# Loading the first nine raw parts of w_in one part per transfer instead of three

## The chip, the cores and the metric

The kernel runs on one core of one Trainium2 chip. The metric is device time in microseconds (us) of one execution. Smaller is better.

## The reference

Two blocks follow each other. The first is a gated delta rule over 4 batches, 8 heads, 768 positions and a head width of 48: for each position the normalised key reads the 48x48 state, and the state gets a rank-one correction.

```
k_n = k / (norm(k) + 1e-6)
for t in range(768):
    y[t]  = q[t] @ state
    v_old = state.T @ k_n[t]
    state = state + beta[t] * outer(k_n[t], v[t] - v_old)
```

The heads are then laid side by side, which gives x with 3072 rows and 384 columns, and the second block is `out = gelu(x @ w_in) @ w_out` with `gelu(h) = h * sigmoid(1.702 h)`. `w_in` is 384x2048 and `w_out` is 2048x384. Both weights arrive as 64-bit floats, because the scale that makes them is a 64-bit number; q, k, v and beta are 32-bit.

## The kernel before

**Tiling.** The 768 positions are cut into 6 chunks of 128, and each pair of chunk and batch is one of 24 units. A unit's keys are turned (`psT`, `kT`), multiplied with each other (`psG`, `G`), and `G` is written to DRAM and read back in another layout (`Nd<-G`, then `NT<-Nd`). `invert` solves the small triangular systems on VectorE: it works in `NT`, `YB` and products `P`, ends in `YS`, and sends that through DRAM too (`Yd<-YS`, then `XB<-Yd`). TensorE uses `XB` in `psU`, ScalarE copies the result to `US`, TensorE makes `psR` from it, and VectorE subtracts `psR` from `V`. That step repeats for four blocks of 32 positions. The results, `xT`, feed the second block: `ph` is x @ w_in, `gT` is its gelu, `po` is the product with w_out.

**Weights.** Each raw 64-bit part is loaded into a place that is not needed yet (the tail of `w_out`, which is why the profile calls its destination `w_out`) and then converted to 32 bits on VectorE by `from_double` (L182 to L194). `w_in` has 12 parts: part `3*g + j` is column group g (512 columns) and contraction third j (128 rows). The list `x_rows` (L204) says how the 128 partitions of one part are filled: partitions 0 to 47, 48 to 63, 64 to 111 and 112 to 127, so four transfers, each with rows of 512 doubles (4 KB). `together_with` (L226) makes the first nine parts travel three at a time: in one call of `fetch` (L234) four transfers load three parts, and within a partition the three parts lie side by side. Parts 9, 10 and 11 travel alone.

**Order of the work around the change.** The loads of the first nine parts are issued by SyncE, from `ahead(1, sync)` (L875, parts 0 to 2, after the keys) and `ahead(2, sync)` (L899, parts 3 to 8, after q, v and more keys and ahead of the first `invert`). `sync` is the pinned form of the SyncE issue: pinned instructions keep the order in which the program names them on their engine. Parts 9 to 11 and all of w_out are issued by GpSimd. Part 0 is converted in L876 on VectorE after `normalize_first` for the first four keys, parts 1 and 2 in L890, then comes the first `invert` (L900), `normalize_first` for three more keys, and the conversion of the next parts (L902 and `weights` in each slot, counts in `WB`). TensorE is kept awake by `warm` matmuls (`ps_warm`) on data that nobody reads. Slots -1 to 5 run `slot`, those from 6 on run `woven`; in slots 2 to 5 VectorE, ScalarE and TensorE instructions are not pinned, and the framework's scheduler sets their order when the program is built.

Of the kernel before, what the change touches and what calls it, by code (L numbers as in the profile page):

```python
# [18 lines left out]
def kernel(  # L19
# [107 lines left out]
    for blk in range(NB):  # L127
# [10 lines left out]
        out=YB, in_=YB, compare_op=ALU.not_equal, fill=1.0, base=0,  # L138
# [27 lines left out]
    def from_double(dst, raw, n, alone):  # L166
# [37 lines left out]
    x_rows = [  # L204
        (ct * DP + o, (ct * NP + i) * D, m, step)
        for ct in range(2)
        for o, i, m, step in ((0, 0, D, D), (D, KC, XR, XR))
    ]
# [3 lines left out]
    def stage(part):  # L212

        if part < parts_in:
            at = part % (2 * KC) * 2 * N_IN
            return at, at + 2 * N_IN
        f = part - parts_in
        if f >= FC - 2:
            return None
        depth = 2 if f < 2 or f >= 8 else 4  # L220
        if f >= 12:
            depth = 1
        at = FC * DM // (2 if f < 2 else 1) - (f % depth + 1) * 2 * DM
        return at, at + 2 * DM

    def together_with(part):  # L226

        return list(range(part, part + (KC if part < 3 * KC else 1)))
# [5 lines left out]
    def fetch(part, dma):  # L234

        if part < parts_in:
            j, f0 = part % KC, part // KC * N_IN
            parts = together_with(part)
            shape, src = (len(parts), N_IN), moe_w_in[:, f0 : f0 + N_IN]
            dst = w_in[:, j : j + len(parts), f0 : f0 + N_IN]  # L240
        else:
            parts = [part]
            shape, src = (1, DM), moe_w_out
            dst = target(part)
        if src.dtype != F32:
            if (s := stage(part)) is None:
                raw = wk.tile([128, *shape, 2], I32, tag="xT", name="raw", bufs=3)
            else:
                words = slice(s[0], stage(parts[-1])[1])
                raw = w_out.rearrange("p f d -> p (f d)")[:, words].bitcast(I32)  # L250
                raw = raw.rearrange("p (j n o) -> p j n o", j=shape[0], o=2)
            for i, p in enumerate(parts):
                stages[p] = raw[:, i]
                if s is not None:
                    taken[p] = stage(p)
            dst = raw.bitcast(src.dtype).rearrange("p j n o -> p j (n o)")
        if part < parts_in:
            for p, r, m, step in x_rows:
                row = src[r + j * step : r + j * step + m]
                dma(  # L260
                    out=dst[p : p + m],
                    in_=bass.AP(
                        row.tensor, row.offset, [row.ap[0], [row.ap[0][0] * step, len(parts)], row.ap[1]]
                    ),
                )
        else:
            r = (part - parts_in) * 128
            dma(out=dst if src.dtype == F32 else dst[:, 0], in_=src[r : r + 128, :])
        return parts

    def target(part):
        if part < parts_in:
            j, f0 = part % KC, part // KC * N_IN
            return w_in[:, j, f0 : f0 + N_IN]
        return w_out[:, part - parts_in, :]
# [394 lines left out]
    def ahead(n, dma=nc.gpsimd.dma_start):  # L670

        while n > 0 and waiting and free(waiting[0]):
            staged.extend(fetch(waiting.pop(0), dma))
            n -= 1
# [228 lines left out]
    for n in range(-1, len(units) + 1):  # L903
        in_order[0], now[0] = n < HB or n >= W, n
        step = slot if n < W else woven
# [32 lines left out]
```

## Time and profile before

| What | Value |
|---|---|
| median of 4 runs | 826.1 us (823.93 to 828.8) |
| the profiled execution's own time | 827.8 us |
| its span | 826.1 us |
| TensorE matmul busy | 771.9 us (93% of the span) |
| VectorE busy | 485.1 us (59%) |
| DMA on SyncE's and ScalarE's queue (q1) | 139488 packets, 41.96 MB, 24.8% of 16 engines |
| w_in loads from SyncE | 6 of 576 KB, 12.2 us to landing; 6 of 192 KB, 12.8 us |
| w_in loads from GpSimd | 6 of 192 KB, 4.4 us; 6 of 64 KB, 4.1 us |

The span runs from the first to the last instruction of the profiled execution; its own time is 1.7 us longer, which lies around the span. A busy share is an average over stages with different limits. TensorE has idle time mostly in the first eighth of the span, where the weights arrive; later it is busy nearly all the time.

### The profile page before, as it was taken

Reading aid. Unit: us, or ns where it says so; the run is one execution under the profiler, and the core shown is the slowest. Engines: PE = TensorE matmul, PEld = TensorE weight load, DVE = VectorE, ACT = ScalarE, POOL = GpSimd, SP = SyncE. Lnnn points to the kernel's source line nnn. Section 1 sums busy time; section 2 is a strip of 40 time slices with the busy share of each in tenths; the row PEclk is TensorE's granted clock in tenths of the full one; section 3 lists DMA queues with packets and bytes.
Section 4 is the critical chain, followed back from the end, with each engine's and each line's share of the span. In section 5 each row is a group of like instructions: output and inputs, shape, how many; then the busy total and the mean of one; then the engine's idle time right before and its main releaser. Section 6 shows DMA issues by size and latency. Waiting matters only on the chain.

```text
span 826.1 us, 18734 instructions
## 1 busy us (share of the span) xinstructions
PE 771.9 (93%) x8100; PEld 581.2 (70%) x8100; DVE 485.1 (59%) x1037; ACT 230.5 (28%) x499; POOL 131.3 (16%) x138
## 2 busy tenths in 40 slices
PE   8438699989989999999999999999999999999998
PEld 7327598556766876876867867867868768677684
DVE  6998889687876665675666667666656730100000
ACT  2303543242322332332322422322322323212120
POOL 2103120242021121222122122112201000000000
PEclk9559988987969999999999999999999999999999
DMA  9996632622124223123214204213222010000000
GB/s 148 201 157 148 171 94 69 174 67 77 46 42 101 53 57 85 38 56 92 62 21 101 62 22 101 53 33 89 52 56 47 11 41 11 11 16 1 24 1 19
DMA packets 147314, 55.96 MB, mean 68 GB/s; under 512 B 114336, under 2 KB 143232, under 8 KB 147232
## 3 DMA queue, kind: packets, MB, share of 16 engines
q1 hardware_dynamic: 139488, 41.96, 24.8%
q0 software_dynamic: 2752, 10.62, 4.3%
q10 hardware_dynamic: 4992, 2.20, 1.0%
q8 instruction: 63, 1.03, 0.5%
q14 instruction: 19, 0.16, 0.1%
HBM read 33.13 MB, written 20.45 MB: 65 GB/s over the span
## 4 chain that ended last, share of the span: by engine, by line
PE 77%; DVE 9%; issue 6%; DMA 5%; POOL 2%; ACT 1%; SPq 0%; DVEq 0%; POOLq 0%; ACTq 0%
PE po L105 28%; PE ph L105 25%; PE psY L105 5%; PE psU L105 4%; PE psQ L105 3%; PE ph L638 3%; DVE P L105 2%; PE psG L105 2%; DMA Nd<-G 2%; PE psR L105 2%; PE ps_warm L154 2%; DVE YB L105 2%; PE psT L105 1%; DMA w_out<-in_moe_w_out_dram 1%; PE psG L367 1%
## 5 line engine op out<-in xcount | busy, mean ns | idle before, releaser
L105 PE MATMUL po<-w_out,gT 128*128 128x384 f32 x704 | 239.3, 490 | 0.0
L105 PE MATMUL ph<-xT,w_in 128*128 128x256 f32 x966 | 222.1, 384 | 0.3
L105 PEld LDWEIGHTS ph<-xT,w_in 128*128 128x128 f32 x966 | 180.3, 191 | 30.9 <-issue 2.3
L105 PEld LDWEIGHTS po<-w_out,gT 128*128 128x128 f32 x704 | 130.1, 190 | 82.6 <-issue 1.9
L105 DVE TENSOR_TENSOR V<-V,psR 64x384 f32<-64x384 f32 (+1 forms) x80 | 44.4, 555 | 192.4 <-PE psR L105 191.6
L105 DVE TENSOR_TENSOR P<-NT,YB 64x18 f32<-64x18 f32 (+25 forms) x171 | 82.3, 481 | 4.5
L105 ACT ACTIVATE gT<-ph 128x512 f32<-128x512 f32 x81 | 48.2, 595 | 115.9 <-PE ph L105 115.8
L105 DVE TENSOR_REDUCE YB<-P 64x6 f32<-64x18 f32 (+25 forms) x171 | 72.6, 425 | 5.5
L105 ACT COPY US<-psU 32x384 f32<-32x384 f32 x80 | 37.6, 470 | 123.7 <-PE psR L105 116.9
L533 POOL TENSOR_SCALAR_AFFINE_SELECT M<-M 128x1024 f32<-128x1024 f32 x24 | 29.8, 1243 | 231.8 <-DVE M L105 162.9
L105 PEld LDWEIGHTS psU<-V,XB 32*32 32x32 f32 x1280 | 45.9, 105 | 29.3 <-issue 21.1
L105 PE MATMUL psU<-V,XB 32*32 32x48 f32 x1280 | 54.5, 203 | 3.7 <-DVE V L105 3.7
L105 PE MATMUL psR<-US,G 32*32 32x48 f32 x1920 | 52.8, 203 | 0.3 <-ACT US L105 0.3
L638 PE MATMUL ph<-xT,w_in 128*128 128x128 f32 (+1 forms) x282 | 51.0, 340 | 1.9 <-DMA xT<-last 1.9
L638 PEld LDWEIGHTS ph<-xT,w_in 128*128 128x128 f32 x282 | 43.6, 212 | 6.6 <-issue 2.9
L105 PEld LDWEIGHTS psR<-US,G 32*32 32x32 f32 x1920 | 44.6, 105 | 1.0 <-issue 0.5
L313 POOL TENSOR_TENSOR rn<-ssq,half 128x8 f32<-128x8 f32 x17 | 37.9, 2229 | 2.9 <-DVE ssq L311 2.9
L154 PE MATMUL ps_warm<-ident 128*128 128x256 bf16 x152 | 22.9, 318 | 16.0 <-DVE ps_warm L105 13.7
L90 POOL DMA_DIRECT2D KN<-in_k_dram x14 | 13.4, 955 | 153.0 <-PE psY L105 101.2
L105 ACT COPY o<-po 128x384 f32<-128x384 f32 x22 | 10.5, 479 | 77.7 <-PE po L105 55.8
L154 PEld LDWEIGHTS <-ident 128*128 128x128 bf16 x152 | 17.1, 114 | 20.4 <-issue 13.9
L105 DVE TENSOR_TENSOR P<-NT 64x256 f32<-64x256 f32 (+7 forms) x36 | 30.6, 849 | 0.3
(144 smaller groups left out, 869.8 us busy)
## 6 DMA issues: line engine op xcount, KB each, us to landing
Nd<-G SPq DMA_DIRECT2D x20, 512.0 KB, 3.5
w_out<-in_moe_w_out_dram POOLq DMA_DIRECT2D x14, 384.0 KB, 3.7
QP<-in_q_dram SPq DMA_DIRECT2D x24, 192.0 KB, 3.9
V<-in_v_dram SPq DMA_DIRECT2D x24, 192.0 KB, 2.9
out_dram<-o SPq DMA_DIRECT2D x24, 192.0 KB, 2.0
w_out<-in_moe_w_in_dram SPq DMA_DIRECT2D x6, 576.0 KB, 12.2
NT<-Nd SPq DMA_DIRECT2D x24, 128.0 KB, 2.7
Yd<-YS SPq DMA_DIRECT2D x24, 128.0 KB, 3.5
```

The costliest lines, as they stand in the source:

```text
L90: dma(out=dst[n % len(dst)][:, :, 0:D], in_=src[b, :, c * C : (c + 1) * C, :].rearrange("h p d -> p h d"),)
L105: return lambda *a, **kw: tc.keep_in_program_order(op(*a, **kw))
L154: pe.matmul(ps, lhsT=ones[:, 0:128], rhs=ones, start=True, stop=True)
L313: nc.gpsimd.tensor_tensor(rn, ssq, half, op=ALU.pow)
L367: pe.matmul(ps[h % 2][:, h // 2], lhsT=kT[r, h // 2, :], rhs=kT[r, h // 2, :], start=True, stop=True,)
L533: nc.gpsimd.affine_select(out=self.M, in_=self.M, compare_op=ALU.is_gt, fill=0.0, base=0, pattern=[[0, H], [1, 128]], channel_multiplier=-1,)
L638: pe.matmul(ph[:, u], lhsT=w_in[:, j, f * 128 : (f + 1) * 128], rhs=xT[:, j, t], start=(j == 0), stop=(j == KC - 1),)
```

## The change

For the parts that travel three at a time, the four transfers that each load three parts are replaced by twelve that each load one part, in the order part by part. The bytes, the rows of 4 KB, the places in SBUF, the issuing engine and the position in the program are the same. For parts 9 to 11 the loop runs once and issues the same four transfers as before.

```diff
         if part < parts_in:
-            for p, r, m, step in x_rows:
-                row = src[r + j * step : r + j * step + m]
-                dma(
-                    out=dst[p : p + m],
-                    in_=bass.AP(
-                        row.tensor, row.offset, [row.ap[0], [row.ap[0][0] * step, len(parts)], row.ap[1]]
-                    ),
-                )
+            for i in range(len(parts)):
+                for p, r, m, step in x_rows:
+                    dma(out=dst[p : p + m, i], in_=src[r + (j + i) * step : r + (j + i) * step + m])
         else:
```

Before, the rows of one partition (one for each of the three parts) follow each other in a transfer; after, each transfer has one row for each partition.

## The prediction

> **What bounds the kernel now.** I read the page's 40 slices first: TensorE stands at 9 tenths nearly everywhere after slice 5, and its gaps lie in the first 100 us, where all nine parts are loaded. So only the end of that opening can move the end of the kernel. I then read the timelines of VectorE, TensorE and SyncE in the two places where SyncE loads w_in, and the stretches of DMA beside them. Columns of a timeline: start, length, engine, line, operation, and in brackets the idle time before it and what ended it.
>
> First load (issued from 4.36 us):
>
> ```profile
> 4.36 2.08 SPq L105 DMA_DIRECT2D w_out<-in_moe_w_in_dram  x4
> 15.61 1.03 DVE L105 TENSOR_TENSOR KN<-KN,z 128x384 f32<-128x384 f32 x2
> 18.73 0.43 DVE L105 TENSOR_SCALAR w_in<-w_out 128x512 int32<-128x512 int32 x1 [2.09 <-DMA w_out<-in_moe_w_in_dram]
> 21.33 6.70 SPq L385 DMA_DIRECT2D NT<-Nd  x4
> 22.91 0.44 ACTq L105 DMA_DIRECT2D Nd<-G  x1
> 30.38 1.23 DVE L105 TENSOR_TENSOR NT<-NT,bI 128x1024 f32<-128x1024 f32 x1 [0.61 <-DMA NT<-Nd]
> ```
>
> VectorE is free at 16.64 and waits 2.09 us for w_in. It converts three parts until 29.77 and then waits again, 0.61 us, for NT. From 30.38 to 57.99 follows the first inversion, VectorE almost without a gap.
>
> Second and third load (issued 38.91 to 44.73):
>
> ```profile
> 38.91 5.82 SPq L105 DMA_DIRECT2D w_out<-in_moe_w_in_dram  x8
> 57.99 1.72 SPq L105 DMA_DIRECT2D Yd<-YS  x4
> 64.03 2.32 SPq L105 DMA_DIRECT2D XB<-Yd  x4
> 64.56 2.13 PE L105 MATMUL ps_warm<-ident 128*128 128x256 bf16 x18
> 66.64 0.86 PE L105 MATMUL psU<-V,XB 32*32 32x48 f32 x16
> 68.85 0.88 PE L105 MATMUL psR<-US,G 32*32 32x48 f32 x48
> 71.29 1.14 DVE L105 TENSOR_TENSOR V<-V,psR 32x384 f32<-32x384 f32 x2
> ```
>
> The loads land 8.9 to 19.5 us after their issue, the last at 63.8. Yd, on the same queue, lands at 64.0 to 64.8 (6.0 to 5.5 us), XB's first at 66.6. In VectorE's timeline there is no idle time from 57.9 to 72.9: three keys are normalised, part 3 and the start of part 4 are converted, and only then comes V.
>
> DMA at three times (columns: stretch, length, busy PE, PEld, DVE, ACT, POOL with counts, PE clock, DMA share, GB/s):
>
> ```profile
> 8.00:10.00 2.00, 2.00 (x20) 1.80 (x19) 1.76 (x9) 0.00 (x0) 0.00 (x0) 1.00 1.00 135
> 52.00:54.00 2.00, 0.00 (x0) 0.00 (x0) 1.97 (x3) 0.00 (x0) 0.00 (x0) 0.50 0.99 158
> 79.00:79.50 0.50, 0.50 (x7) 0.45 (x6) 0.50 (x2) 0.13 (x1) 0.50 (x2) 1.00 0.99 291
> ```
>
> The first two are loads of three parts, the third is a part that travels alone, from GpSimd's queue. All have 4 KB rows and engines busy throughout, yet the third moves about twice as much.
>
> [...] the 576 KB transfers run at 135 to 158 GB/s, those of 192 KB at 291. [...]
>
> **The change part by part.**
>
> *Transfer rate.* It gains. A part is 128 x 4 KB = 524 KB. Lower bound of the gain: none (150 GB/s stays, since SyncE's queue may not do what GpSimd's does); upper: 291. I take 291. The first load then flows from about 8.0 us, when the keys are in, for 1573 KB / 291 = 5.4 us and lands near 14.9 (1.5 us from the last byte to landing: the bytes ended at 17.0, the landing is 18.6) instead of 18.6. The second and third flow from about 42.5 for 10.8 us, landing near 55 instead of 63.8.
>
> *First stall.* The 2.09 us before the conversion go, at either rate: at 150 GB/s part 0 alone would land at 8.0 + 3.5 + 1.5 = 13.0, before VectorE is free at 16.64. VectorE then ends its conversions at 27.7. **NT is late next.** NT's last read is issued at 27.72, when the last Nd has landed, and lands 2.5 us later. Nd's last write starts at 22.91, as soon as ScalarE has copied G, behind TensorE and the normalised keys; none of that reads w_in. Nor do they share DMA: between 17.0 and 18.0 the engines are nearly idle (share 0.16 and 0.01), and the first Nd moves only from 18.3. So NT's arrival stays, the 0.61 us wait grows to 2.7, and the gain is 0.0. Bounds: 0 to 0.6 us; the whole 0.61 is had only if Nd comes sooner.
>
> *Issues on SyncE.* 8 more in the first load and 16 more in the other two, 0.436 us each by the median of the w_in rows: 3.5 us and 7.0 us. The first ends near 10 us; next on SyncE is NT at 21.33, which waits for Nd: hidden, with 11 us left. The others end near 51.7; next is Yd at 57.99, which waits for YS: hidden, 6.3 us left. If that cover were gone, Yd would be late one for one.
>
> *Eight transfers in flight.* After its eight issues SyncE's queue shows one wait of 3.1 us for a w_in load, from 44.73 to 47.8: exactly when the first of the eight landed, before it went on to wait 10.1 us for YS. I read this as: the ninth transfer waits for the landing of the first. Then the new loads wait for those eight ahead, so two parts are in flight. GpSimd's single transfers land after 3.6 to 4.7 us, which allows 1049 KB / 4.4 = 238 GB/s: 3146 KB in 13.2 us, until 55.7 and landed by 57.2, still ahead of Yd. At 150 GB/s part 7 would land near 61 and hold Yd's issue for 3 us; but Yd's bytes queue behind w_in to 62 today too, so it would land as it does now. Cost 0; bounds 0 to 0.6.
>
> *Yd and XB.* With w_in gone, Yd takes its usual 3.5 us (the page's median), XB is issued near 61.5 and its first lands near 64.1, 2.5 us sooner. **The warm matmuls are next.** TensorE runs them without a gap from 56.82 to 66.5, in pinned order ahead of psU; the wait for XB there is 0.2 us. So psU gains 0.2 us, and even that is lost at V, which waits for VectorE until 71.29 while psR ends near 69.7. Gain 0.0; bounds 0 to 0.2.
>
> *Conversions of parts 3 to 8* never wait for a load in the trace (the first is at 65.7); GpSimd's loads of parts 9 to 11 wait for VectorE to free their place (22.5 us at 68.44). Nothing moves.
>
> Sum: 0 + 0 + 0, with 0 to -0.8 from the covered pieces; I take -0.2. On the profiled execution's own time that is 827.8 to 827.6. That execution lies 1.7 above the median of 826.1, so the forecast is 825.9.
>
> **The rivals.**
>
> *Both stalls were real.* If NT came earlier with w_in, or the warm matmuls gave way, the end would gain 0.6 + 2.5 and, if VectorE's 2.09 us counted fully, up to 5 us: 821. For it: the chain of waits names Yd (5.49 us from 59.29). Against: VectorE has no gap there, so that piece is a bookkeeping of equals.
>
> *Another order in slots 2 to 5 (and of unpinned transfers elsewhere).* The scheduler sees twelve transfers where there were four and may place unpinned work differently between about 100 and 230 us. It decides when an Nd, NT, Yd or XB falls behind another unpinned transfer on SyncE that waits. Its price is read from waits of that region: psU waited 4.0 us for the XB issued at 226.77, and six xT transfers in a row hold the queue for 5.07 us. One such slip costs 4 to 5 us with TensorE otherwise full: 830.5, **slower**. It decides only where it puts more than the present wait ahead of psU. A lucky order removes the 4.0 us instead: 822. Nothing in the profile shows that the order will change.
>
> *The change doesn't speed the loads.* Then Yd lands as now, and the first stall still goes: 826.1, the same class.
>
> **How the numbers follow.** A difference under 0.5% (4.1 us) is about what a measurement of this kernel can tell from no change. Covered pieces as worked out, or no faster loads: 0.62. Faster by more than 4.1: 0.21 (0.10 both stalls real, 0.11 a better order). Slower by more than 4.1: 0.17, by order, with a few hundredths for Yd held on SyncE past 65. The likeliest case's own range is 823.5 to 828.5; the range to 8 in 10 reaches into both orders, 820.5 to 831.
>
> **What would show it.** Right: w_in transfers from SyncE landing in 4 to 7 us, DMA near 250 to 290 GB/s at 9 to 13 and 43 to 55 us, no wait for w_in before the first conversion but about 2.7 us for NT at 30.4; YS still at 56.7; Yd landing in about 3.5 us; psU still at 66.4 to 66.7, V at 71.3. Wrong: NT's product before 29.9, or psU before 66, or V before 71; SyncE's w_in issues past 58; or another order of instructions after 100 us.

## The result and the profile after

The changed kernel takes 823.1 us at the median of 43 runs (819.4 to 830.6), the kernel before 826.7 us of 64 runs (822.1 to 833.4). The ratio is 0.9959 with a 95% interval of 0.9945 to 0.9973: 3.4 us gained, 2.2 to 4.5. (The median of before was 826.1 when four runs were known.) Ratios and averages leave out the few runs that fell in a slower state of the chip. The profiled execution of after took 823.39 us with a span of 821.3 us, against 827.8 and 826.1 before. The mean granted clock is 0.952, against 0.948.

SyncE's timeline of after (start, length, engine, line, operation), as the prediction showed it of before:

```profile
4.25 6.80 SPq L105 DMA_DIRECT2D w_out<-in_moe_w_in_dram  x12
20.19 8.04 SPq L380 DMA_DIRECT2D NT<-Nd  x4
38.94 15.53 SPq L105 DMA_DIRECT2D w_out<-in_moe_w_in_dram  x24
58.66 1.71 SPq L105 DMA_DIRECT2D Yd<-YS  x4
60.64 2.66 SPq L105 DMA_DIRECT2D XB<-Yd  x4
```

XB is issued 3.4 us sooner than before (64.03), because Yd no longer lands behind w_in (1.9 to 2.3 us after its issue in place of 5.5 to 6.0). The DMA stretches of after (length, busy engines with counts, PE clock, DMA share, GB/s):

```profile
8.00:10.00 2.00, 2.00 (x21) 1.79 (x19) 1.76 (x9) 0.00 (x0) 0.00 (x0) 1.00 1.04 234
52.00:54.00 2.00, 0.00 (x0) 0.00 (x0) 2.00 (x4) 0.26 (x1) 0.00 (x0) 0.50 1.02 213
```

The DMA engines are as busy as before and move 234 GB/s in place of 135, and 213 in place of 158. Stretches of 2 us scatter; from 9 to 13 us it is 228 in place of 147, from 44 to 54 us 215 in place of 155. TensorE's clock is 1.00 in the first of the two stretches, where warm matmuls keep it busy for all 2.00 us, and 0.50 in the second, where it runs nothing. VectorE's timeline of after, in the opening:

```profile
16.52 0.42 DVE L105 TENSOR_SCALAR w_in<-w_out 128x512 int32<-128x512 int32 x1
...
30.45 1.22 DVE L105 TENSOR_TENSOR NT<-NT,bI 128x1024 f32<-128x1024 f32 x1 [2.89 <-DMA NT<-Nd]
...
53.23 0.42 DVE L182 TENSOR_SCALAR w_in<-w_out 128x512 int32<-128x512 int32 x1
...
57.41 1.23 DVE L456 TENSOR_TENSOR YS<-YB,bI 128x1024 f32<-128x1024 f32 x1
...
63.20 0.17 DVE L105 TENSOR_SCALAR z<-z 128x24 f32<-128x24 f32 x1
63.28 0.69 DVE L193 SCALAR_TENSOR_TENSOR w_in<-w_out,w_in 128x512 int32<-128x512 int32 x1
...
65.15 0.69 DVE L194 SCALAR_TENSOR_TENSOR w_in<-tmp,w_in 128x512 f32<-128x512 f32 x1
...
69.57 1.14 DVE L105 TENSOR_TENSOR V<-V,psR 32x384 f32<-32x384 f32 x2
```

The first conversion waits for nothing, and NT's product starts when it did before: the first stall went and came back as a wait of 2.89 us for NT. What is new stands at 53.23 to 65.15: ten conversion instructions of parts 3 and 4 (lines L182 and L191 to L194) now lie inside the tail of the first inversion and between the small instructions of `normalize_first`. Before, they came after the keys, in front of V:

```profile
65.72 0.76 DVE L182 TENSOR_SCALAR w_in<-w_out 128x512 int32<-128x512 int32 x2
...
70.56 0.69 DVE L194 SCALAR_TENSOR_TENSOR w_in<-tmp,w_in 128x512 f32<-128x512 f32 x1
```

V is 1.7 us sooner (71.29 before), though the same instructions stand ahead of it. In before the small instructions on `z`, each of which needs the result of the one ahead, start about 0.22 us apart (61.58, 61.80, 62.02); in after an independent conversion starts 0.08 us behind such an instruction (63.20 and 63.28). From the product P at 52.4 us to V it is 18.9 us in before and 17.2 in after. The price is that YS, with two conversions ahead of it, starts 0.7 us later (57.41, 56.73 before). TensorE, ScalarE and GpSimd issue the same instructions in the same order as before, VectorE all but those ten.

From 75 to 124 us after is ahead by 1.2 to 1.6 us, at the end of the span by 4.8. Nearly all of the rest of this pair of profiles arises in one place, between 124 and 135 us. TensorE's timeline of before and then of after, at the first products of x with w_in:

```profile
126.48 0.89 PE L638 MATMUL ph<-xT,w_in 128*128 128x128 f32 x4 [1.94 <-DMA xT<-last]
127.59 1.22 PE L638 MATMUL ph<-xT,w_in 128*128 128x128 f32 x4
```

```profile
123.65 0.68 PE L633 MATMUL ph<-xT,w_in 128*128 128x128 f32 x4 [0.53 <-DMA xT<-last]
124.89 0.68 PE L633 MATMUL ph<-xT,w_in 128*128 128x128 f32 x4 [0.36 <-DMA xT<-last]
125.70 2.05 PE L633 MATMUL ph<-xT,w_in 128*128 128x128 f32 x16
```

The second four products take 0.68 us in after and 1.22 us in before, where a wait of 1.94 us came first. The windows of 124 to 134 us, before and then after (the PE clock is the third number from the right):

```profile
124.00:134.00 10.00, 8.06 (x63) 6.88 (x63) 9.84 (x18) 3.40 (x8) 0.54 (x1) 0.66 0.34 88
```

```profile
124.00:134.00 10.00, 9.64 (x105) 8.53 (x105) 9.87 (x18) 3.49 (x8) 0.54 (x1) 1.00 0.23 61
```

TensorE ran two thirds of this stretch at half clock in before and none of it in after. Between 80 and 250 us every half-clock stretch of every profile here is a multiple of 3.41 us long (3.41, 6.83, 10.24, 13.65), and within before as within after all of them begin and end on one grid of that step. The stretch here, in before, follows a wait of 1.94 us and lasts 6.83 us, from 126.83 to 133.66.

### The profile page after: what moved, and what is told of

Read it like the earlier page. It is cut to its first block, busy times and chain, and to the rows that moved or that the text cites. A ratio compares the mean times of both kernels' runs of the same rounds, so it can differ in the third digit from the quotient of the medians.

```text
span 821.3 us, 18780 instructions
## 1 busy us (share of the span) xinstructions
PE 767.6 (93%) x8100; PEld 577.8 (70%) x8100; DVE 483.1 (59%) x1037; ACT 231.0 (28%) x499; POOL 133.7 (16%) x138
## 4 chain that ended last, share of the span: by engine, by line
PE 77%; DVE 9%; issue 6%; DMA 5%; POOL 1%; ACT 1%; SPq 0%; DVEq 0%; POOLq 0%; ACTq 0%
PE po L105 28%; PE ph L105 25%; PE psY L105 5%; PE psU L105 4%; PE psQ L105 3%; PE ph L633 3%; DVE P L105 2%; PE psG L105 2%; PE psR L105 2%; DMA Nd<-G 2%; PE psT L105 1%; DVE YB L105 1%; DMA w_out<-in_moe_w_out_dram 1%; PE ps_warm L154 1%; DMA KN<-in_k_dram 1%
## 5 line engine op out<-in xcount | busy, mean ns | idle before, releaser
L105 PE MATMUL po<-w_out,gT 128*128 128x384 f32 x704 | 239.3, 490 | 0.0
L105 PEld LDWEIGHTS po<-w_out,gT 128*128 128x128 f32 x704 | 130.2, 190 | 82.7 <-issue 1.9
L105 DVE TENSOR_TENSOR V<-V,psR 64x384 f32<-64x384 f32 (+1 forms) x80 | 44.4, 555 | 195.2 <-PE psR L105 194.4
L633 PE MATMUL ph<-xT,w_in 128*128 128x128 f32 (+1 forms) x282 | 49.0, 330 | 0.9 <-DMA xT<-last 0.9
L308 POOL TENSOR_TENSOR rn<-ssq,half 128x8 f32<-128x8 f32 x17 | 39.8, 2343 | 2.9 <-DVE ssq L306 2.9
L650 PE MATMUL po<-w_out,gT 128*128 128x384 f32 x64 | 26.8, 553 | 4.0 <-DVE w_out L194 4.0
```

Of the source, the lines that this page charges most:

```text
L105: return lambda *a, **kw: tc.keep_in_program_order(op(*a, **kw))
L308: nc.gpsimd.tensor_tensor(rn, ssq, half, op=ALU.pow)
L633: pe.matmul(ph[:, u], lhsT=w_in[:, j, f * 128 : (f + 1) * 128], rhs=xT[:, j, t], start=(j == 0), stop=(j == KC - 1),)
L650: pe.matmul(po, lhsT=gT[f // FQ][:, f % FQ, i * C : (i + 1) * C], rhs=w_out[:, f, :], start=(f == 0), stop=(f == FC - 1),)
```

## The experiments

The theory going in was that the gain is V's 1.7 us, and so the new order on VectorE. The first rival: the speed of the loads gains by itself. The second, formed after the first four runs: the gain is the half clock behind the wait at 124 us.

All runs at a glance. The ratio is to before in the same comparison; V is its first start in the profile; "half" is the half-clock time between 80 and 250 us by the trace's clock records; "xT" is TensorE's longest wait for xT near 124 us, and the clock beside it that of 124 to 134 us. "Planner's" is the order that the build gives when warm matmuls are added.

| Kernel | w_in loads 0-2 / 3-8 | order on VectorE | median us | ratio (95%) | span | V | half | xT, clock |
|---|---|---|---|---|---|---|---|---|
| before | three / three | before | 826.7 | 1 | 826.1 | 71.3 | 47.8 | 1.9, 0.66 |
| after | one / one | after | 823.1 | 0.9959 (0.9945-0.9973) | 821.3 | 69.6 | 41.0 | 0.5, 1.00 |
| after_again | one / one | after | 824.1 | 0.9966 (0.9952-0.9979) | 821.0 | 69.7 | 41.0 | 1.2, 1.00 |
| order_only | three / three | after | 826.9 | 1.0001 (0.9978-1.0023) | 824.1 | 71.7 | 37.5 | 1.8, 0.83 |
| fast_only | one / one | before | 822.7 | 0.9953 (0.9930-0.9976) | 823.9 | 71.7 | 44.4 | 1.9, 0.83 |
| fast_again | one / one | before | 825.4 | 0.9982 (0.9962-1.0002) | 820.8 | 71.9 | 37.5 | 1.0, 1.00 |
| split_first | one / three | before | 824.6 | 0.9977 (0.9957-0.9997) | 819.8 | 72.2 | 30.7 | 1.0, 1.00 |
| split_rest | three / one | after | 823.5 | 0.9968 (0.9945-0.9990) | 825.7 | 70.1 | 47.8 | 1.2, 1.00 |
| near_rows | three, near rows | before | 828.0 | 1.0001 (0.9980-1.0023) | 824.8 | 71.2 | 41.0 | 2.3, 0.83 |
| cut_rows | three, cut | before | 832.6 | 1.0079 (1.0052-1.0106) | 830.9 | 82.1 | 47.8 | shifted |
| fill_gap | three / three | planner's | 823.8 | 0.9971 (0.9954-0.9989) | 820.3 | 71.7 | 41.0 | 0.3, 1.00 |
| fill_gap_after | one / one | planner's | 822.8 | 0.9952 (0.9933-0.9970) | 820.0 | 70.7 | 41.0 | under 0.7, 1.00 |
| fill_late | one / one | planner's | 818.4 | 0.9899 (0.9861-0.9938) | 821.4 | 70.8 | 34.1 | 1.8, 0.83 |
| fill_all | one / one | planner's | 820.2 | 0.9925 (0.9892-0.9957) | 818.6 | 70.4 | 17.1 | under 0.7, 1.00 |

**The order alone, and the loads alone.** order_only keeps the three-part loads and names the ten instructions in the places that after gives them; fast_only is after with them named where before has them.

```diff
 # order_only, on before: called after the given VectorE instruction of the first inversion and keys
+    hooks[44] = [piece(3, 182)]
+    hooks[46] = [piece(3, 193)]
...
+    hooks[58] = [piece(4, 194)]
 # fast_only, on after: called behind the keys
+    piece(3, 182)()
+    piece(4, 182)()
...
+    piece(4, 194)()
```

> The loads of the kernel before (three parts per transfer), with the ten VectorE conversions of parts 3 and 4 written into the places that they have in the changed kernel. Theory A (the gain comes from the new VectorE order): the time falls as with the whole change, ratio 0.996 to 0.998; part 3 lands near 54.1 here, so the first moved conversion (at 53.2 in the changed kernel) waits up to 0.9 us, and V comes at 70 to 70.5 instead of 71.3. Theory B (the gain comes from the earlier landing of w_in and Yd): no gain, ratio 1.000, V not before 71.

> The loads of the changed kernel (one part per transfer), with the VectorE conversions of parts 3 and 4 held in the order of the kernel before, behind the normalised keys. Theory A: ratio 0.999 to 1.001; the first stall moves from w_in to NT (about 2.9 us at 30.4) and V stays at 71.2 to 71.4. Theory B: ratio 0.996, as with the whole change, and V near 69.6.

> The whole change once more, beside the other kernels on this chip. Both theories: ratio 0.9959, V near 69.6. In its trace the clock of TensorE should stay full between 124 and 134 us if the gain there belongs to the change; if it drops to half as in the kernel before, part of the difference between the two first traces was the state of one execution.

The order alone gains nothing (1.0001). VectorE's timeline of order_only shows why V does not come sooner:

```profile
54.95 0.43 DVE L108 TENSOR_SCALAR w_in<-w_out 128x512 int32<-128x512 int32 x1 [1.15 <-DMA w_out<-in_moe_w_in_dram]
59.14 1.22 DVE L513 TENSOR_TENSOR YS<-YB,bI 128x1024 f32<-128x1024 f32 x1
71.69 1.14 DVE L108 TENSOR_TENSOR V<-V,psR 32x384 f32<-32x384 f32 x2 [0.41 <-PE psR L108]
```

With slow loads part 3 isn't there when the order wants it; this wait and the two conversions ahead of YS put it 2.4 us later than in before (56.73), Yd and XB with it, and V waits for psR. So this run doesn't price the order beside fast loads. The loads alone do gain, with V at 71.7. So the theory that V and the order make the gain fell. One profile could not have told: fast_only's profiled execution, with a span of 823.9 us, lay among the slower of its runs (819.7 to 830.4 us).

**A second sample.** fast_again is fast_only once more.

> fast_only once more (loads part by part, VectorE in the order of before), for a second profile and a second sample. If its gain is real: 821.5 to 824.5 us, with V again at about 71.7 us, so the gain does not come by way of V; the time then lies between 120 and 260 us, where the half-clock stretches are. If the first sample was a lucky one: about 826 us, as V says.

It came out between the two: 0.9982, where the first sample had 0.9953. Weighted by their intervals the two give 0.9970 (0.9954 to 0.9985), 2.5 us gained with V where it was before. The two profiles of this one kernel are 3.1 us apart in span, V 0.2 us apart, half-clock time 6.8 us apart. Half of 6.8 us, an estimate of the work lost in them, is 3.4 us: enough for the whole difference. So two executions of one kernel differ by as much as the change gains, and only the timed runs carry a verdict here.

**The granted clock of every run.** Each timed run has its span and its mean granted clock on record, and from the two the time at half clock follows. (The clock records of before and after hold two values only, 1.0 and 0.5, so a mean clock of 0.95 over 824 us means a tenth of them, 82 us, at half clock.) It is 82.7 us on average in 156 runs of before and 79.7 in the 66 of after and after_again. These 3.0 us (interval 1.5 to 4.5) are worth an estimated 1.5 us at most (the same four products took 1.22 us at half clock and 0.68 at full), while the mean span is 3.2 us shorter. Runs of the same clock differ too: at 0.952 the spans of after average 820.8 us and those of before 823.8, at 0.950 822.1 and 824.3. So by the middle values less half clock explains at most about half of the gain; the rest would be work that starts sooner. (A mean over a run doesn't say where its half clock fell.)

**Which loads.**

```diff
+            if part == 0:     # split_first; split_rest has: if part >= KC
+                for i in range(len(parts)):
+                    for p, r, m, step in x_rows:
+                        dma(out=dst[p : p + m, i], in_=src[r + (j + i) * step : r + (j + i) * step + m])
+            else:
...
```

> Only the first load (parts 0 to 2) part by part; parts 3 to 8 as three-part loads; every engine but SyncE in the order of before. If the gain comes from the loads of parts 3 to 8 and what follows them (Yd and XB sooner, the conversions of parts 3 and 4 inside the first inversion's tail), nothing is gained: about 826.7 us, first landing at about 15 us, XB issued at about 63 us, V at about 71.3 us. If the first load carries it (VectorE without its 2 us wait for w_in at 18.9 us), about 823.5 us. My guess: 826.5.

> Only the loads of parts 3 to 8 part by part, the first as before; every engine but SyncE in the order of after. If these loads carry the gain: about 823.3 us, VectorE still waiting about 2 us for w_in at 18.9 us, V at about 69.6 us, the PE's wait for xT<-last near 124 us 1 us or less and no half-clock stretch at 127 to 133 us. If the first load is needed too, between 824.5 and 826.7 us.

Each half alone gains, 0.23% and 0.32%, and both together 0.34 to 0.41%: less than their sum by the middle values, though the intervals are too wide to exclude it. My guess for split_first (826.5) missed. Its profile has V at 72.2, later than before, and no half clock at 124 to 134 us. The pair also shows what made the new order: split_rest is built with the VectorE order of after, split_first with that of before. The order follows from the loads of parts 3 to 8. And each load's rate follows its own form, in one execution: split_first moves 217 GB/s from 9 to 13 us and 156 from 44 to 54, split_rest 146 and 227.

**What makes the three-part loads slow.** near_rows keeps the three-part transfers, but reads rows of DRAM that lie beside each other (16 KB apart) for the three rows of a partition, so the product is that of a w_in with its rows permuted. cut_rows makes as many transfers as after, but cuts them along the partitions: three rows still go to each.

```diff
-                        row.tensor, row.offset, [row.ap[0], [row.ap[0][0] * step, len(parts)], row.ap[1]]
+                        row.tensor, row.offset, [[row.ap[0][0] * len(parts), m], [row.ap[0][0] * (1 if len(parts) > 1 else step), len(parts)], row.ap[1]]
 # cut_rows
+                w = -(-m // len(parts))
+                for a in range(0, m, w):
+                    cut = row[a : min(a + w, m)]
+                    dma(out=dst[p + a : min(p + a + w, p + m)], in_=...)
```

> The loads of the kernel before, but the three rows that follow each other into one partition are neighbouring rows of w_in (16 KB apart) instead of rows 48 (or 16) apart; the rows of w_in thus go to other partitions, so the product is that of a permuted w_in. If packets that follow each other into one partition are what is slow: still 135 to 160 GB/s at 44 to 60 us and landings of 9 to 19 us. If the distance of the rows in DRAM is what is slow: 250 to 290 GB/s and landings of 4 to 8 us. The time: 1.000 by theory A, since the VectorE order is that of the kernel before.

> As many transfers as in after (24 more on SyncE, most of 192 KB), but cut along the partitions: each still brings three rows into one partition, so packets that follow each other still go to the same one. Every engine but SyncE has the order of before. If the succession of packets makes the three-part loads slow: 135 to 165 GB/s while they run, first landing at about 18.6 us, second and third at 61 to 64 us, 826 to 827.5 us. If it is the size or the number of the transfers: 200 GB/s or more, landing at 14.9 and 55 us, and about 823.5 us.

The stretches of near_rows, then of cut_rows:

```profile
8.00:10.00 2.00, 2.00 (x21) 1.80 (x19) 1.73 (x9) 0.00 (x0) 0.00 (x0) 1.00 1.05 131
52.00:54.00 2.00, 0.00 (x0) 0.00 (x0) 1.97 (x3) 0.00 (x0) 0.00 (x0) 0.50 1.05 182
```

```profile
8.00:10.00 2.00, 2.00 (x21) 1.79 (x20) 1.73 (x9) 0.00 (x0) 0.00 (x0) 1.00 0.96 133
52.00:54.00 2.00, 0.00 (x0) 0.00 (x0) 1.86 (x5) 0.00 (x0) 0.00 (x0) 0.50 0.66 117
```

The distance of the rows in DRAM isn't it (131 against 135 GB/s in the first load, 162 against 155 from 44 to 54 us, and no change in time). Nor does it help to make many small transfers: cut_rows is slow too. That leaves the three rows in turn for one partition, the only thing after changes that neither of these does, but cut_rows is no clean price for it. Its groups have 4 to 16 partitions, and from 52 to 54 us, in the second load, the DMA share is 0.66 (1.02 in after, 0.99 in before); why it is lower was not shown. Per busy engine an estimate of 117 / 0.66 = 177 stands against after's 213 / 1.02 = 209, and lies among the 159 to 191 that the uncut three-part loads of before, near_rows, order_only and split_first give by the same working.

Both times that I expected for cut_rows missed: it is 0.79% slower. VectorE and SyncE show it:

```profile
29.54 0.43 DVE L105 TENSOR_SCALAR w_in<-w_out 128x512 int32<-128x512 int32 x1 [12.71 <-DMA NT<-Nd]
```

```profile
4.47 19.42 SPq L105 DMA_DIRECT2D w_out<-in_moe_w_in_dram  x12
68.84 1.73 SPq L105 DMA_DIRECT2D Yd<-YS  x4
```

SyncE takes 19.4 us for twelve issues, VectorE waits 12.7 us before the first conversion (the view names NT; the instruction reads the w_in load), and V is 10.9 us late. Of that only 6.5 us reach the time and 4.8 the span. That is about 0.6 us of time for one of V. By this rough rate, from one run in which other waits moved too, V's 1.7 us are worth an estimated 1.0 us, under a third of the 3.4 gained.

**The wait at 124 us and the half clock.** fill_gap puts warm matmuls where TensorE waits for xT, without any change to the loads; fill_gap_after does the same to after.

```diff
+            if (n, group) == (3, 0):
+                warm(18)
```

> The kernel before with 18 warm matmuls more, queued on the PE where it waits 1.9 us for xT<-last at 126 us (some 29 VectorE instructions and some matmuls after that point also change places, put there by the kernel's own planner). If the half clock from 127 to 133 us follows from that wait, it is gone: the 16 products of the expert layer there take 2.05 us as in after and not 3.78, and the time is 2 to 3.5 us under before, 823.2 to 824.7 us. [...]

> after with the 18 warm matmuls of fill_gap in the same place (the kernel's planner moves the same 29 VectorE instructions and some matmuls). If the gain of after is mostly the half clock at 127 to 133 us that fill_gap removes as well, the two don't add: 822.5 to 824 us. If the faster loads gain by another way, they add to fill_gap's 2.2 us: 820 to 821.5 us.

The windows of fill_gap:

```profile
124.00:134.00 10.00, 9.68 (x110) 8.64 (x109) 9.84 (x18) 3.54 (x8) 0.54 (x1) 1.00 0.28 82
```

The half clock is gone from this stretch and 2.4 us are gained with the old loads. On after the same edit brings the ratio from 0.9959 and 0.9966 to 0.9952, not to the 0.993 that the sum of both gains would give. So the two gains seem to be largely the same one; the interval, to 0.9933, just reaches full addition, and some 29 VectorE instructions moved along with the edit in both, so this is support and no proof.

**A version that beats both.** TensorE waits 4.2 us for XB at 221 us in after, in front of the longest half-clock stretch. fill_late puts 34 warm matmuls there, fill_all also 28 at 95 us and 18 at 124 us.

```diff
+            if (n, group) == (5, 5):
+                warm(34)
```

> after with 34 warm matmuls on the PE where it waits 4.2 us for V at 221 us, in front of the longest half-clock stretch after 80 us (13.7 us in every profile of a kernel so far). If that idle time brings the half clock: the stretch goes or shrinks to 7 us or less, and 3 to 6 us are gained, 817.5 to 820.5 us. If VectorE sets the pace there and the PE only waits longer, 822.5 to 824.5 us.

> after with warm matmuls in three of the PE's waits: 28 at 95 us, 18 at 124 us, 34 at 221 us (the planner then orders the conversions of w_out and some matmuls otherwise). If each wait brings its half clock and the gains add: 814 to 818 us, half-clock time between 80 and 250 us under 25 us (41 in after). If the waits merely move: 822 to 826 us.

The windows of 224 to 238 us, of after and then of fill_late:

```profile
224.00:238.00 14.00, 12.07 (x163) 10.48 (x164) 8.86 (x23) 3.08 (x8) 2.83 (x3) 0.52 0.21 39
```

```profile
224.00:238.00 14.00, 13.77 (x213) 11.46 (x212) 9.81 (x34) 4.66 (x11) 2.04 (x3) 1.00 0.33 62
```

The stretch runs at full clock and the kernel takes 818.4 us, 0.9899 of before (0.9861 to 0.9938, from six runs): the fastest of all. By the same count as above its six runs have 65 us at half clock on average, against 80 in after. (The profiled execution, at 823.6 us, is the slowest of the six.) The edit also moved 14 VectorE instructions and one of ScalarE. TensorE's timeline of fill_late shows that it has no idle time left there:

```profile
225.21 3.88 PE L154 MATMUL ps_warm<-ident 128*128 128x256 bf16 x34
229.12 0.86 PE L548 MATMUL psU<-V,XB 32*32 32x48 f32 x30
```

The XB that psU needs was issued at 224.1 and 224.6 and landed 2.7 to 2.9 us later, by 227.5. So the last of the warm matmuls held psU back by up to 1.6 us, and fewer may gain more; that was not tried.

fill_all missed its 814 to 818 us. It has the least half-clock time of all (17.1 us) and still is no faster than fill_late: with three blocks of warm matmuls the planner moves dozens of VectorE instructions, and other waits grow, such as that for KN, 2.4 us at 243 us (1.5 us in fill_late). Half-clock time alone doesn't give the time: fill_all has 17.1 us of it and takes 820.2 us, fill_late 34.1 and 818.4.

## Why the prediction was right or wrong

The range (820.5 to 831.0) held the time, and the likeliest class, within 0.5%, was the right one: 0.41% faster, interval 0.27 to 0.55. In part that was luck: a gain of 0.2 us was forecast and 3.4 were had, close under the edge of the class. The number, 825.9, was 2.8 us too high, and two steps failed.

- **Transfer rate: right in kind, too high.** 291 GB/s was taken from a stretch of 0.5 us; from 79 to 81 us GpSimd's load in before runs at 238, and after's loads run at 234 and 213. Landings take 3.9 to 6.3 us, as forecast (4 to 7). The last load is issued at 54.2 and lands at 58.0, not near 55, and still in time for Yd.
- **First stall: right.** The 2.09 us went, NT was late next, with a wait of 2.89 us (forecast 2.7), and its product stood at 30.45 (30.38 before). Gain 0.
- **Issues on SyncE, eight in flight: right that they are hidden.** They end at 11.05 and 54.47, not 10 and 51.7, because SyncE waits for landings in part of the 15.5 us: of the 24 issues from 38.94 us on, the ninth to the seventeenth each start within 0.1 us of the landing of the one eight ahead (the ninth at 45.26, the first lands at 45.24), as the prediction had read it. Yd comes at 58.66.
- **Yd and XB: right on psU, not on YS.** YS starts at 57.41 and not at 56.7, since two conversions moved ahead of it. Yd lands in 1.9 to 2.3 us, XB is issued at 60.64, and psU starts at 66.36, 0.28 us sooner (bound 0.2), because the warm matmuls are next.
- **Conversions of parts 3 to 8, "Nothing moves": wrong.** Those of parts 3 and 4 are placed by the scheduler, and with sooner loads it placed them ahead of the normalised keys. So V moved from 71.29 to 69.57, though the text held it at 71.3 and named a V before 71 as a sign of being wrong. At 69.57 it stands right behind psR, which ends at 69.45. I had considered another order, but only after 100 us, where in fact nothing changed.
- **The sum: a term was missing.** I summed waits and had no term for the granted clock, although the profile page's row of it and the half-speed stretches after 100 us were there to be read. TensorE "at 9 tenths nearly everywhere" is busy time, not work: the same products count for 1.22 us at half clock and 0.68 at full. Of the eight profiles that have before's uncut loads or faster ones and no filling, three have 3.41 us of half clock there, before 6.83: between 124 and 135 us they gain 1.2 to 1.7 us on before. The five with none gain 3.5 to 4.1 us, of which 0.7 to 1.4 come from the shorter wait for xT itself. Before's profile is the worst of them there, so the pair overstates this part; over all runs less half clock is worth at most about 1.5 us. The premise that only the end of the opening can move the end of the kernel fell with it: most of what this pair gains arises behind 100 us.

Of the rivals, the lucky order came nearest in time (822), but it was to remove the wait of 4.0 us for XB near 227 us, and that wait stands, 4.2 us in after. "Both stalls were real" (821) had the wrong mechanism: neither NT nor psU moved. That the change doesn't speed the loads is refuted by the rates. No transfer slipped on SyncE.

**What is shown and what stays open.** Shown by timed runs: faster loads gain with the old order, the new order doesn't with the old loads, either half of the loads gains, and filling the wait at 124 us gains about as much without touching the loads. Less half clock is at most about half of the gain; how the rest divides between V and shorter waits isn't shown. Not shown either is how loads that end by 60 us shorten a wait at 124 us. There is only a correlation: all three profiles with the uncut three-part loads and no filling have a wait of 1.8 us or more and half clock there, of six profiles with faster loads one has. fill_late, whose loads are those of after, has it too, so the same loads can fall on either side. In the four profiles with the uncut three-part loads (fill_gap's among them), SyncE starts the second of the six xT transfers 1.02 to 1.04 us after the first, in eight with faster loads 0.60 to 0.61; what causes these 0.4 us was not tried. In cut_rows, whose loads are slow but as many as after's, it is 0.61 too, so this gap goes with the number of transfers and not with their landing. A second candidate stands beside it: GpSimd issues a 384 KB load of w_out, once VectorE has freed its place, between the same six transfers. Of the profiles without filling at 124 us, in those with a wait of 1.8 us or more only two or three xT transfers were issued before it, in those with 1.2 us or less four (in split_rest the fourth came 0.01 us after it). In fast_only it came 1.39 us after the first xT, in fast_again, the same kernel, 2.23. No run moved that load. How three rows in turn for one partition come to load at a lower rate wasn't shown either.

## What to carry to other kernels

When a profile shows busy time, multiply it by the granted clock before calling a stretch full (four products took 1.22 us at half clock and 0.68 at full): waits of about 2 us were followed here by 3.4 to 6.8 us of half clock, an estimated 1.7 to 3.4 us of work at most, and filler work in a wait was the best edit of this study (fill_late, 0.9899). An edit to a load can change the order of instructions that aren't pinned (ten conversions moved here), so ask which of those that read the load the scheduler may place elsewhere. Where single executions of one kernel differ by 3 us, take the verdict from many runs and a profile for the mechanism only, and compare the clock over all runs before one pair of profiles is made the whole story.

## What the runs showed of the hardware that was not expected

- Loads of the same bytes and rows of 4 KB differ in rate, with the order of the rows and the size of a transfer, while the DMA share is the same (1.01 in before and 1.04 in after from 9 to 13 us): from 9 to 13 and from 44 to 54 us 134 to 162 GB/s in the uncut profiles with three rows in turn for each partition, 200 to 228 GB/s with one (before, near_rows, order_only and fill_gap; after, after_again, fast_only, fast_again and the two split kernels).
- Cutting a transfer into groups of 4 to 16 partitions kept three rows in turn and left the DMA engines at a share of 0.66 in the second load: 117 GB/s, and SyncE took 19.4 us for twelve issues.
- Each wait for xT of 1.8 us or more at 124 us was followed by half clock, those of 1.2 us or less weren't. What the step of the 3.41 us grid around the wait holds tells more. In the five profiles that lose the clock there without filling at 124 us, TensorE is busy for 1.14 to 1.73 us of that step (1.47 in before); in the five that keep it (fast_again, split_rest, after_again, split_first, after) for 1.92 to 2.52 us. fill_all is the exception: it stands idle for 1.9 us at 125 us, ahead of psU, is busy for 1.57 us of the step, and keeps the full clock until 168 us. Over all profiles, from 64 to 250 us, each of the 33 full-clock steps with TensorE busy for under 40% was followed by half clock, and none of the 412 with over 90% (in before and after alone 6 and 59); between the two both occur (there 5 of 18 were).
- The half clock behind the 4.2 us wait at 221 us lasted 13.65 us in after, and filling that wait took the time from 823 to 818 us.
